# Two-token K/Q pieces, a mask added by TensorE and a new order, in sliding-window attention followed by a squared-ReLU MoE layer

## The chip, the cores and the metric

The kernel runs on one core of one Trainium2 chip. A core has TensorE (PE in the profile; PEld is its loading of weights), VectorE (DVE), ScalarE (ACT), GpSimd (POOL) and SyncE (SP). They run side by side and wait for each other by semaphores. Loads and stores go through 16 DMA engines, which all queues share. POOL, SP and ACT issue them; only those that POOL issues convert float32 to bfloat16 on the way here. The metric is the device time of one execution in microseconds (us), the median over runs.

## The reference

```python
def _attn_ref(q, k, v):                     # 8 batches, 8 heads, 576 tokens, 64 per head
    scores = scale * np.matmul(q, k.transpose(0, 1, 3, 2))          # scale = 1/8
    mask = np.abs(pos[:, None] - pos[None, :]) <= window            # window = 32
    scores = np.where(mask, scores, -1000000000.0)
    ...
    attn = attn / (np.sum(attn, axis=-1, keepdims=True) + 1e-09)    # softmax
    return np.matmul(attn, v)

def _moe_ref(x, w_in, w_out):               # x: 4608 x 512, w_in: 512 x 2048
    r = np.maximum(x @ w_in, 0.0)
    return (r * r) @ w_out
```

Attention gives 4608 tokens (8 batches of 576) with 512 features each, heads side by side, and these go through the two products. Inputs and output are float32.

## The kernel before

**Steps and tiles.** A batch is cut into nine steps of 64 queries, 72 steps in all. A step sees 128 keys, from 32 before its queries to 32 behind them. Its scores for all eight heads fill one PSUM bank, 128 keys by 512 (line 552; two banks, `sc`, taken in turn). ACT takes the exponential (line 562), DVE multiplies by a mask of 0 and 1 (line 569), PE multiplies with V (AV, line 585) where a column of ones beside V gives the sum, DVE divides (lines 597 and 599), and the result `xr` is turned into `xt`: by PE and ACT in the first 26 steps (lines 619 and 624), by a DMA afterwards (line 610).

Eight steps make a tile of 512 tokens, nine tiles in all. In a tile the first product, mm1 (line 629), makes the hidden layer in 16 units. A unit fills one of two PSUM banks, `ht`, in turn, so that a unit waits until ACT has taken the unit before the last from its bank; ACT applies the ReLU and DVE or ACT squares (lines 648 and 655), giving `gt`. From tile 2 on a unit is 128 features by 512 tokens, 8 matmuls of 64 rows. In tile 0 it is 256 features by 256 tokens, 16 matmuls, in the order of the list `UNITS`, whose entries are (first token, tokens, first block of 128 features); in tile 1 it is the same size, first half first. The second product, mm2 (line 662), goes through 128 tokens in four units of 8 matmuls, one for each fourth of the hidden layer (`seg`), into one of two banks, `outp`. Four loads bring w_in and four bring w_out, 512 hidden features each: blocks 0 to 3 of a unit's third entry need w_in chunk 0, and so on.

**How Q, K and V get in.** For batches 2 to 7, K and Q are loaded by heads (line 434), turned in blocks by DVE (line 492) and spread by SP's DMAs (line 506). Batches 0 and 1 take a faster way in `PIECES` of 128 tokens and a last one of 64: `fine_load` (line 388) puts one token of all heads on a partition, so that a run is 64 numbers; `fine_turn` turns it by PE with an identity (line 405), and ACT or DVE copy it from PSUM: K once (line 416), Q twice, each with half of the rows zeroed (lines 423 and 424). The first piece of batch 0 comes in float32 by SP's and ACT's queues into a part of `gt` not used yet, the others by POOL. V comes in four pieces of 128 tokens, shifted by 32, and two edges (lines 443 and 451); DVE makes a second copy for the even steps (line 463).

**What sets the order.** `Prog` records every operation with what it reads and writes, a key (its due time, in steps) and an estimated duration. Then `schedule` plays the program through and lets each engine, when it is free, take the ready operation with the smallest key. The order found is emitted as each engine's program; on the chip it is fixed, and an engine waits where an operation isn't ready. The keys come from the tables at the head: `LEAD`, `LB`, `TB`, `GB`, `QB`, `WB`, `VB` for the batches, `KM`, `TM`, `MD` for mm1 and mm2. `FIRST` lists the first 40 loads (K, Q, V, V edges, w_in as `a`, w_out as `b`) in the order in which POOL issues them, ahead of all others. `AHEAD` limits how many of POOL's loads may be under way: an issue waits for an earlier load where more than that many nanoseconds of transfer, by the plan's estimate, lie ahead. In time without other work PE multiplies a tile of zeros, `zz`, into an unused bank, to keep its clock up.

Of the kernel before, what the change touches and what calls it, by code (L numbers as in the profile page):

```python
# [5 lines left out]
ALU = mybir.AluOpType  # L6
ACTF = mybir.ActivationFunctionType
BF16 = mybir.dt.bfloat16
# [12 lines left out]
LEAD = 13  # L21
# [16 lines left out]
NG, GK = 72, -5.5  # L38
WIDE = (0,)
W1F = ()  # L40
QENG = 'AAAADDDDDA'
# [9 lines left out]
FIRST = (  # L51
# [6 lines left out]
)  # L58
WCH = ((0, 512), (512, 512), (1024, 512), (1536, 512))
PIECES = ((0, 128), (128, 128), (256, 128), (384, 128), (512, 64))  # L60
# [225 lines left out]
class Gen:  # L286
# [5 lines left out]
    def alloc(self):  # L292
# [14 lines left out]
        self.FR = {t: [sb(f"{t}fr{i}", [128, 5, H_, D_], BF16) for i in range(2)] for t in "qk"}  # L307
# [15 lines left out]
        self.FF = {t: wide[:, x:x + 1024].rearrange("p (x h d) -> p x h d", x=2, h=H_) for t, x in (("k", 2048), ("q", 3072))}  # L323
# [44 lines left out]

    def setup_rest(self, i, key):

        self.ms("DVE", [("vx0", i)], self.VX[i][64:96, 0, :, 0:64], 0.0, key, 280)
        self.ms("DVE", [("vx0", i)], self.VX[i][64:128, 0, :, 64:VS], 1.0, key, 80)
        self.ms("DVE", [("vx4", i)], self.VX[i][32:64, 4, :, 0:64], 0.0, key, 280)
        self.ms("DVE", [("vx4", i)], self.VX[i][0:64, 4, :, 64:VS], 1.0, key, 80)
# [5 lines left out]

    def fine_load(self, b, t, x, key):
        t0, n = PIECES[x]
        s = (self.q if t == "q" else self.k)[b][:, t0:t0 + n, :].rearrange("h p d -> p h d")
        d = self.FR[t][b][0:n, x, :, :]
        on = "POOL"
        if b == 0 and x in WIDE:
            d, on = self.FF[t][:, x, :, :], "ACT" if t == "q" else "SP"
        self.p.rec(on, lambda e: e.dma_start(d, s), writes=[("fraw", b, t, x)], dma=(f"f{b}{t}{x}", 0), key=key,  # L388
                   dur=(900 if n == 128 else 700) if on == "POOL" else 450, move=(n // 2, 14 if on == "POOL" else 16))

    def fine_turn(self, b, t, x, key):

        t0, n = PIECES[x]
        tag, ps = ("sc", t == "q"), self.SC[t == "q"]
        if b == 0 and x < 4:
            tag, ps = (("ht", x % 2), self.HT[x % 2][:]) if t == "q" else (("outp", 0), self.OUTP[0][:])
        wide = b == 0 and x in WIDE
        raw, ident, turned = (self.FF[t], self.IF, False) if wide else (self.FR[t][b], self.ID, n == 128)
# [10 lines left out]
        self.p.rec("PE", f, reads=[("fraw", b, t, x), "idf" if wide else "id"] + [("frz", b, t)] * (n < 128), writes=[tag], key=key,  # L409
                   dur=(232 if n == 128 else 120) * (4 if wide else 1),  # L410
                   mode="col")
        src = ps[:, 0:4 * n].rearrange("p (j c) -> p j c", j=4)
        if t == "k":
            dst = self.KT[b][:, :, 32 + t0:32 + t0 + n]
# [3 lines left out]
                       dur=(430 if n == 128 else 430) if on == "DVE" else (600 if n == 128 else 390))  # L418
            return
        for hm in range(2):  # L420
            dst, on = self.QZ[b][:, :, hm, t0:t0 + n], "DVE" if QENG[5 * b + x] == "D" else "ACT"
# [4 lines left out]
                       dur=(690 if n == 128 else 480) if on == "ACT" else (480 if n == 128 else 430))  # L426
# [29 lines left out]
    def copy_v(self, b, key, s0, s1):  # L456
# [4 lines left out]
        for r in (0, 64):  # L461
            dst, src = self.VX[i][r:r + 64, s0 + r // 64:s1 + r // 64, :, :], self.VD[i][r:r + 64, s0:s1, :, :]
# [33 lines left out]
    def spread(self, b, t, dh, key):  # L496
        st, i = self.ST[t], b % 2
        rd = [("st", t, dh, m0) for m0 in (0, 3, 5, 7)]
        old = [(t + "f", b - 2, x, hm) for x in range(5) for hm in range(2)] if b < 4 else []
# [10 lines left out]
    def qk_tags(self, b, c):  # L510
# [3 lines left out]
        if b < 2:  # L514
            for x in range((64 * c) // 128, min(575, 64 * c + 95) // 128 + 1):
                rd += [("kf", b, x, 0)]
# [299 lines left out]
```

## Time and profile before

| | us |
|---|---|
| median of three runs | 313.03 |
| the three runs | 310.76, 313.03, 314.44 |
| profiled execution | 312.9 |
| its span, first to last instruction | 311.1 |
| PE busy | 298.4 |
| DVE busy | 191.1 |
| ACT busy | 188.0 |
| POOL busy | 88.3 |

The granted TensorE clock was 1.000 over the span. The profile shows one execution. In its rows, "L67 PE MATMUL ht<-xt,w" is line 67 of the kernel, run on PE, that writes `ht` and reads `xt` and the weights; x and a number is how many there were. A row of a stretch of time gives the engine's busy time in it and the number of its instructions. In the page's second part a digit is a busy share in tenths for a fortieth of the span. Matmuls overlap, so that a busy PE isn't one at its peak.

### The profile page before, as it was taken

Reading aid. Unit: us, or ns where it says so; the run is one execution under the profiler, and the core shown is the slowest. Engines: PE = TensorE matmul, PEld = TensorE weight load, DVE = VectorE, ACT = ScalarE, POOL = GpSimd, SP = SyncE. Lnnn points to the kernel's source line nnn. Section 1 sums busy time; section 2 is a strip of 40 time slices with the busy share of each in tenths; the row PEclk is TensorE's granted clock in tenths of the full one; section 3 lists DMA queues with packets and bytes.
Section 4 is the critical chain, followed back from the end, with each engine's and each line's share of the span. In section 5 each row is a group of like instructions: output and inputs, shape, how many; then the busy total and the mean of one; then the engine's idle time right before and its main releaser. Section 6 shows DMA issues by size and latency. Waiting matters only on the chain.

```text
span 311.1 us, 9658 instructions
## 1 busy us (share of the span) xinstructions
PE 298.4 (96%) x4087; PEld 210.3 (68%) x4087; DVE 191.1 (61%) x485; ACT 188.0 (60%) x349; POOL 88.3 (28%) x127
## 2 busy tenths in 40 slices
PE   7799978999999999999999999999999999999996
PEld 3467967878867577677767776666666666565555
DVE  7865766877788788887858763869555440232000
ACT  3575776756746793588357868867786543253211
POOL 8837656973543242431141031000000000000000
PEclk9999999999999999999999999999999999999999
DMA  9999999999999979997799395434331110100112
GB/s 133 138 186 165 146 196 186 181 236 216 229 126 219 141 90 164 232 170 94 137 181 206 70 105 73 69 86 93 96 70 53 34 54 36 67 36 34 70 75 95
DMA packets 99226, 38.77 MB, mean 125 GB/s; under 512 B 71920, under 2 KB 94192, under 8 KB 99184
## 3 DMA queue, kind: packets, MB, share of 16 engines
q0 software_dynamic: 71584, 18.10, 63.1%
q1 hardware_dynamic: 21520, 10.63, 15.5%
q10 hardware_dynamic: 6080, 9.44, 9.9%
q8 instruction: 32, 0.52, 0.7%
q14 instruction: 10, 0.08, 0.1%
HBM read 36.70 MB, written 9.44 MB: 148 GB/s over the span
## 4 chain that ended last, share of the span: by engine, by line
PE 83%; DMA 9%; POOL 3%; issue 2%; ACT 1%; DVE 1%; SPq 0%; POOLq 0%; ACTq 0%
PE ht L67 38%; PE outp L67 37%; PE sc L552 4%; DMA xt<-xr 3%; PE ta L585 2%; DMA kfr<-in_k_dram 2%; DMA qz<-qst 2%; DMA qfr<-in_q_dram 2%; POOL vd L443 1%; POOL qfr L388 1%; POOL kfr L388 1%; ACT rt L648 1%; PE sc L405 1%; PE ta L619 1%; SPq L506 0%
## 5 line engine op out<-in xcount | busy, mean ns | idle before, releaser
L67 PE MATMUL ht<-xt,w 128*64 128x512 bf16 (+1 forms) x1408 | 140.5, 342 | 1.8 <-DMA xt<-xr 0.7
L67 PE MATMUL outp<-w,gt 128*64 128x512 bf16 (+1 forms) x1184 | 139.1, 373 | 0.0
L648 ACT ACTIVATE rt<-ht 128x512 bf16<-128x512 f32 x144 | 85.1, 596 | 56.7 <-PE ht L67 50.4
L67 PEld LDWEIGHTS ht<-xt,w 128*64 128x64 bf16 x1408 | 93.9, 137 | 31.5 <-issue 2.0
L67 PEld LDWEIGHTS outp<-w,gt 128*64 128x64 bf16 x1184 | 71.4, 110 | 38.2
L655 DVE TENSOR_TENSOR gt<-rt 128x512 bf16<-128x512 bf16 x94 | 38.9, 424 | 47.3 <-ACT rt L648 29.1
L562 ACT ACTIVATE e<-sc 128x512 bf16<-128x512 f32 x72 | 41.7, 598 | 8.6 <-PE sc L552 7.0
L676 ACT ACTIVATE oe<-outp 128x512 f32<-128x512 f32 x35 | 20.8, 595 | 37.7 <-PE outp L67 37.7
L443 POOL DMA_DIRECT2D vd<-in_v_dram x32 | 28.5, 893 | 45.7 <-PE ta L585 34.6
L492 DVE STREAM_TRANSPOSE qst<-qraw 128x256 bf16<-128x256 bf16 (+1 forms) x48 | 35.8, 830 | 1.7 <-DMA qz<-qst 1.7
L492 DVE STREAM_TRANSPOSE kst<-kraw 128x256 bf16<-128x256 bf16 (+1 forms) x48 | 35.9, 830 | 0.6 <-DMA kt<-kst 0.6
L597 DVE RECIPROCAL rs<-ta 128x4 f32<-128x4 f32 x72 | 13.0, 180 | 33.2 <-PE ta L585 32.7
L655 ACT ACTIVATE gt<-rt 128x512 bf16<-128x512 bf16 x50 | 31.6, 631 | 0.9
L569 DVE TENSOR_TENSOR pt<-e,mask 128x512 bf16<-128x512 bf16 x72 | 29.2, 410 | 4.4 <-ACT e L562 3.8
L599 DVE TENSOR_TENSOR xr<-ta,rs 128x256 bf16<-128x256 f32 x72 | 30.4, 422 | 0.9
L552 PE MATMUL sc<-qz,kt 128*64 128x128 bf16 x576 | 26.5, 219 | 2.6 <-issue 1.1
L552 PEld LDWEIGHTS sc<-qz,kt 128*64 128x64 bf16 x576 | 22.1, 110 | 8.1 <-issue 2.3
L434 POOL DMA_DIRECT2D qraw<-in_q_dram x24 | 15.2, 635 | 12.1 <-DVE qst L492 4.8
L451 POOL DMA_DIRECT2D vx<-in_v_dram x16 | 9.4, 590 | 27.1 <-PE ta L585 14.7
L434 POOL DMA_DIRECT2D kraw<-in_k_dram x24 | 14.5, 607 | 7.2 <-DVE kst L492 4.2
L463 DVE COPY vx<-vd 64x528 bf16<-64x528 bf16 (+1 forms) x28 | 14.7, 525 | 1.7 <-DMA vd<-in_v_dram 1.1
L585 PEld LDWEIGHTS ta<-vx,pt 128*64 128x64 bf16 x320 | 11.7, 111 | 5.2 <-issue 1.0
(53 smaller groups left out, 133.9 us busy)
## 6 DMA issues: line engine op xcount, KB each, us to landing
out_dram<-oe ACTq DMA_DIRECT2D x35, 256.0 KB, 3.1
vd<-in_v_dram POOLq DMA_DIRECT2D x32, 128.0 KB, 5.3
kraw<-in_k_dram POOLq DMA_DIRECT2D x24, 144.0 KB, 5.1
qraw<-in_q_dram POOLq DMA_DIRECT2D x24, 144.0 KB, 5.1
kt<-kst SPq DMA_DIRECT2D x48, 72.0 KB, 4.4
qz<-qst SPq DMA_DIRECT2D x48, 72.0 KB, 3.8
w<-in_moe_w_in_dram POOLq DMA_DIRECT2D x4, 512.0 KB, 8.4
w<-in_moe_w_out_dram POOLq DMA_DIRECT2D x4, 512.0 KB, 7.7
```

The lines of the kernel that those rows point to most:

```text
L67: mm = e.matmul(out[r:r + 64], w[:, r:r + 64], x, start=start, stop=stop)
L434: self.p.rec("POOL", lambda e, g=g, s=s: e.dma_start(raw[32 * g:32 * g + 32], s), writes=[("raw", t, b % 2, g)], dma=(f"{t}{b % 2}", b), k ...
L443: self.p.rec("POOL", lambda e, s=s: e.dma_start(self.VD[i][:, s, :, 0:64], v[b, :, 32 + 128 * s:160 + 128 * s, :].rearrange("h p d -> p h ...
L492: self.p.rec("DVE", lambda e: e.transpose(dst, src), reads=[("raw", t, i, g) for g in range(4)], writes=[("st", t, dh, m0)], key=key, dur= ...
L552: mm = e.matmul(sc[64 * u:64 * u + 64, 128 * j:128 * j + 128], self.KT[i][:, j, at:at + 64], self.QZ[i][:, j, :, 64 * c:64 * c + 64], star ...
L562: self.p.rec("ACT", lambda e: e.activation(ex, sc, ACTF.Exp, scale=0.125), reads=tags, writes=[("e", n % 4)], key=key, dur=600)
L569: self.p.rec("DVE", lambda e: e.tensor_tensor(pt, ee, mb, ALU.mult), reads=[("e", n % 4), ("mask", mi)], writes=[("pt", n % 4)], key=key, ...
L585: mm = e.matmul(self.PAIR[1][64 * u:64 * u + 64, 1, VE * j:VE * j + VE], pt[:, p0 + 64 * u * w:p0 + 64 * u * w + 64], vt[:, h, 0:VE], star ...
L599: self.p.rec("DVE", lambda e: e.tensor_tensor(bass.AP(xr, o, [[512, 128], [64, 4], [1, 64]]), bass.AP(self.PAIR[1], 512, [[1024, 128], [VE ...
L648: relu = self.p.rec("ACT", lambda e: e.activation(rt[:], ht[:], ACTF.Relu), reads=[("ht", k % 2)], writes=[("rt", k % 4)], key=key, dur=600)
L655: op = self.p.rec(on, lambda e: e.tensor_tensor(dst, rr, rr, ALU.mult) if on == "DVE" else e.activation(dst, rr, ACTF.Square), reads=[("rt ...
L676: self.p.rec("ACT", lambda e: e.activation(oe[:], op[:], ACTF.Copy), reads=[("outp", x % 2)], writes=[("oe", x % 3)], old=[("mtmp", 0), (" ...
```

## The change

K and Q of batches 0 and 1 come in three pieces of 128, 256 and 192 tokens. In the second and third a partition takes two tokens that follow each other, so a run is 128 numbers; PE turns the even and the odd tokens apart, and the copies from PSUM put them back in order. In the first nine steps (`NM`) PE writes a mask into the score bank first, 0 where a key is seen and −8e9 elsewhere (it is made from the masks by DVE and lies in `gt` until tile 1 needs the place), and adds the scores to it, so that the exponential gives the masked value at once and DVE's product is left out. The units of tile 1 have 512 tokens. The ones beside V are written once for all of `vx`, and the copies of V leave them alone. `FIRST`, `UNITS` and the tables of keys are new throughout.

```diff
-LEAD = 13
+LEAD = 2
...
-AHEAD = 5000
-LB = (-12.25, 1.5, 5.25, 2.5, 2.25, 10.75, 9.75, 11.25)
-TB = (22.5, -12.5, -8.5, -2.0, 13.0, 21.5)
-GB = (107.0, 61.0, 77.0, 134.0, 59.0, 9.0)
-TST, SK = 0.05, -10.5
-QB = (53.0, 15.0, -22.0, -4.0, 78.0, 126.0)
-WB = (-54.0, 16.0, 7.0, 75.0, 52.0, 128.0)
-VB = (43.5, -4.5, 36.5, -7.5, -19.0, 29.0)
-SQ = (12, 112, 2)
+AHEAD = 6000
+LB = (-8.5, -3.0, 3.25, 12.0, 1.75, 0.5, 7.0, 15.5)
+TB = (6.0, -7.5, -17.5, -25.0, 8.5, 67.5)
+GB = (223.0, 29.0, 45.0, 118.0, 26.0, 23.0)
+TST, SK = 0.15, -30.5
+QB = (24.0, -19.0, -63.0, 51.0, 51.0, 103.0)
+WB = (-31.0, 160.0, 81.0, 15.0, -4.0, 187.0)
+VB = (52.0, 3.0, 8.5, -58.5, 8.5, 24.5)
+SQ = (8, 112, 2)
...
+T1N = 512
+NM, MK = 9, 21.5
...
-FK, FQ = 41.75, 29.75
-VK0, VK1 = 5.75, 18.25
-KM, MD, TM = -34.5, 22.875, 4.0
+FK, FQ = 40.5, 15.0
+VK0, VK1 = -16.25, 1.0
+KM, MD, TM = -76.0, 21.625, 5.0
 UNITS = (
-    (256, 256, 4), (0, 256, 4), (256, 256, 0), (0, 256, 10), (256, 256, 8), (0, 256, 6), (256, 256, 2),
-    (0, 256, 0), (0, 256, 8), (256, 256, 6), (256, 256, 14), (0, 256, 2), (0, 256, 12), (256, 256, 12),
-    (256, 256, 10), (0, 256, 14),
+    (256, 256, 2), (0, 256, 4), (256, 256, 14), (256, 256, 4), (0, 256, 2), (0, 256, 0), (0, 256, 10),
+    (256, 256, 0), (0, 256, 6), (0, 256, 12), (256, 256, 10), (256, 256, 8), (0, 256, 8), (256, 256, 12),
+    (0, 256, 14), (256, 256, 6),
 )
 FIRST = (
-    ("q", 0, 1), ("v", 0, 1), ("q", 0, 3), ("v", 0, 2), ("v", 0, 3), ("k", 0, 1), ("e", 0, False),
-    ("v", 0, 0), ("q", 0, 4), ("k", 0, 2), ("q", 0, 2), ("q", 0, 0), ("k", 0, 3), ("q", 1, 1), ("a", 0, 1),
-    ("a", 0, 2), ("k", 0, 4), ("a", 0, 0), ("q", 1, 0), ("a", 0, 3), ("k", 1, 0), ("k", 1, 2), ("e", 0, True),
-    ("e", 1, False), ("v", 1, 1), ("v", 1, 0), ("k", 1, 4), ("k", 1, 1), ("b", 0, 1), ("q", 1, 2),
-    ("e", 1, True), ("v", 1, 2), ("k", 1, 3), ("b", 0, 0), ("b", 0, 2), ("q", 1, 3), ("k", 0, 0), ("b", 0, 3),
-    ("q", 1, 4), ("v", 1, 3),
+    ("e", 0, True), ("k", 1, 0), ("q", 0, 1), ("v", 0, 0), ("k", 0, 1), ("e", 0, False),
+    ("v", 0, 1), ("q", 0, 2), ("q", 1, 0), ("v", 0, 2), ("k", 0, 2), ("a", 0, 0), ("k", 0, 0),
+    ("v", 0, 3), ("a", 0, 1), ("e", 1, False), ("q", 1, 1), ("k", 1, 1), ("v", 1, 0),
+    ("a", 0, 3), ("b", 0, 0), ("v", 1, 2), ("q", 0, 0), ("b", 0, 3), ("a", 0, 2), ("q", 1, 2), ("v", 1, 1),
+    ("v", 1, 3), ("e", 1, True), ("k", 1, 2), ("b", 0, 1), ("b", 0, 2),
 )
...
-PIECES = ((0, 128), (128, 128), (256, 128), (384, 128), (512, 64))
+PIECES = (((0, 128, 1), (128, 256, 2), (384, 192, 2)), ((0, 128, 1), (128, 256, 2), (384, 192, 2)))
...
+    def setup_negs(self, key):
+        for i, (t, o) in enumerate(self.NEG):
+            dst = bass.AP(t, o, [[8192, 128], [1, 64]])
+            self.p.rec("DVE", lambda e, i=i, d=dst: e.tensor_scalar(d, self.MASK[i][:], -1.0, 8.0e9, ALU.add, ALU.mult),
+                       reads=[("mask", i)], writes=[("neg", i)], key=key, dur=90)
...
     def fine_load(self, b, t, x, key):
-        t0, n = PIECES[x]
-        s = (self.q if t == "q" else self.k)[b][:, t0:t0 + n, :].rearrange("h p d -> p h d")
+        t0, n, r = PIECES[b][x]
+        s = (self.q if t == "q" else self.k)[b][:, t0:t0 + n, :].rearrange("h (p r) d -> p h (r d)", r=r)
...
     def fine_turn(self, b, t, x, key):
...
         def f(e):
-            for j in range(4):
-                for u in range(2):
-                    h = 4 * (j // 2) + j % 2 + 2 * u
-                    mm = e.matmul(ps[64 * u:64 * u + 64, n * j:n * j + n], raw[:, x, h, :], ident[:, 0:n],
-                                  start=True, stop=True, is_transpose=turned)
+            for c in range(r):
+                for j in range(4):
+                    for u in range(2):
+                        h = 4 * (j // 2) + j % 2 + 2 * u
+                        o = m * (r * j + c)
+                        mm = e.matmul(ps[64 * u:64 * u + 64, o:o + m], raw[:, h, 64 * c:64 * c + 64], ident[:, 0:m],
+                                      start=True, stop=True, is_transpose=turned)
             return mm
...
-        src = ps[:, 0:4 * n].rearrange("p (j c) -> p j c", j=4)
+        src = ps[:, 0:4 * m * r].rearrange("p (j c i) -> p j i c", j=4, c=r)[:, :, 0:n // r, :]
...
     def copy_v(self, b, key, s0, s1):
...
-            dst, src = self.VX[i][r:r + 64, s0 + r // 64:s1 + r // 64, :, :], self.VD[i][r:r + 64, s0:s1, :, :]
+            dst, src = self.VX[i][r:r + 64, s0 + r // 64:s1 + r // 64, :, 0:64], self.VD[i][r:r + 64, s0:s1, :, 0:64]
...
     def scores(self, n):
...
+            if n < NM:
+                t, o = self.NEG[mi]
+                neg = bass.AP(t, o, [[8192, 128], [0, 8], [1, 64]])
+                self.p.rec("PE", lambda e: matmul(e, "col", sc.rearrange("p (h q) -> p h q", h=8), self.ID, neg, True, False),
+                           reads=["id", ("neg", mi)], writes=tags, key=key - MK, dur=240, move=2, mode="col")
...
-                                      self.QZ[i][:, j, :, 64 * c:64 * c + 64], start=True, stop=True)
+                                      self.QZ[i][:, j, :, 64 * c:64 * c + 64], start=n >= NM, stop=n >= NM or j == 3)
...
+        if n < NM:
+            pt = self.PT[n % 4][:]
+            self.p.rec("ACT", lambda e: e.activation(pt, sc, ACTF.Exp, scale=0.125),
+                       reads=tags, writes=[("pt", n % 4)], key=key, dur=600)
+            return
...
             key = 8 * T + d / 2 + TM - 8
-            if T == 1:
+            if T == 1 and T1N == 256:
                 self.mm1(T, 256 * (d // 8), 256, 2 * (d % 8), key)
```

More of the change, by code (lines that the diff above doesn't have):

```diff
@@ L386, in fine_load @@
-        if b == 0 and x in WIDE:
-            d, on = self.FF[t][:, x, :, :], "ACT" if t == "q" else "SP"
+        t0, n, r = PIECES[b][x]
+        s = (self.q if t == "q" else self.k)[b][:, t0:t0 + n, :].rearrange("h (p r) d -> p h (r d)", r=r)
+        d, on = self.piece(b, t, x)[0:n // r], "POOL"
+        if b == 0 and x in WIDE and r == 1:
+            d, on = self.FF[t], "ACT" if t == "q" else "SP"
         self.p.rec(on, lambda e: e.dma_start(d, s), writes=[("fraw", b, t, x)], dma=(f"f{b}{t}{x}", 0), key=key,
-                   dur=(900 if n == 128 else 700) if on == "POOL" else 450, move=(n // 2, 14 if on == "POOL" else 16))
+                   dur=(900 if n // r > 64 else 700) if on == "POOL" else 450,
+                   move=(n // r // 2, (14 if r == 1 else 22) + 2 * (on != "POOL")))
@@ L399, in fine_turn @@
+        turned = not wide and n != 64
+        m = n if n == 64 else 128
+        raw, ident = (self.FF[t], self.IF) if wide else (self.piece(b, t, x), self.ID)
         ps = ps.bitcast(BF16) if turned else ps
         def f(e):
-            for j in range(4):
-                for u in range(2):
-                    h = 4 * (j // 2) + j % 2 + 2 * u
-                    mm = e.matmul(ps[64 * u:64 * u + 64, n * j:n * j + n], raw[:, x, h, :], ident[:, 0:n],
-                                  start=True, stop=True, is_transpose=turned)
@@ L413, in fine_turn @@
+            return mm
+        self.p.rec("PE", f, reads=[("fraw", b, t, x), "idf" if wide else "id"] + [("frz", b, t)] * (n // r < 128), writes=[tag],
+                   key=key, dur=(232 * r if n > 64 else 120) * (4 if wide else 1), move=8 * r, mode="col")
+        src = ps[:, 0:4 * m * r].rearrange("p (j c i) -> p j i c", j=4, c=r)[:, :, 0:n // r, :]
         if t == "k":
-            dst = self.KT[b][:, :, 32 + t0:32 + t0 + n]
+            dst = self.KT[b][:, :, 32 + t0:32 + t0 + n].rearrange("p j (i c) -> p j i c", c=r)
@@ L498, in spread @@
         rd = [("st", t, dh, m0) for m0 in (0, 3, 5, 7)]
-        old = [(t + "f", b - 2, x, hm) for x in range(5) for hm in range(2)] if b < 4 else []
+        old = [(t + "f", b - 2, x, hm) for x in range(3) for hm in range(2)] if b < 4 else []
         for s in range(2):
@@ L656, in mm1 @@
                    reads=[("rt", k % 4)], writes=[("gt", T % 2, d0 + d, u) for d in range(nd) for u in us], key=key,
[L657 removed]
+                   old=["wf"] + [("fraw", 0, t, x) for t in "kq" for x in WIDE] + [("neg", i) for i in range(4)] if T == 1 else [],
                    dur=430 if on == "DVE" else 600)
@@ L757, in build @@
                     self.copy_v(1, n - LEAD - VK1, c, c + 1)
-                if b < 2 and (c % 2 or not c):
-                    x = (c + 1) // 2
-                    if x < 5:
+                for x, (t0, _, _) in enumerate(PIECES[b] if b < 2 else ()):
+                    if c == max(0, t0 // 64 - 1):
                         self.fine_turn(b, "k", x, n - LEAD - FK)
```

56 lines of the change are left out of this document (28 added, 28 removed).

## The prediction

> **What bounds the kernel now.** I read the page first, then the windows of the large matmuls, then the DMA and POOL rows of the start, then the waits and the chain. The page:
>
> ```profile
> PE 298.4 (96%) x4087; PEld 210.3 (68%) x4087; DVE 191.1 (61%) x485; ACT 188.0 (60%) x349; POOL 88.3 (28%) x127
> PE   7799978999999999999999999999999999999996
> DMA  9999999999999979997799395434331110100112
> ```
>
> PE is busy for 96% of 311.1 us, but not with products at first. Below, one row a stretch (length, PE busy, count in brackets, granted clock, DMA): the idle matmuls on the zero tile in the first row, and behind the dots all matmuls that touch the weights (both MoE products).
>
> ```profile
> 0.00:23.00 23.00, 10.92 (x55) 1.00 1.64 152
> ...
> 0.00:23.00 23.00, 1.18 (x18) 1.00 1.64 152
> 23.00:31.00 8.00, 4.84 (x80) 1.00 1.67 167
> 31.00:39.00 8.00, 6.93 (x118) 1.00 1.65 145
> 60.00:100.00 40.00, 37.86 (x420) 1.00 1.45 204
> 150.00:200.00 50.00, 46.50 (x397) 1.00 0.92 122
> ```
>
> Two stages. From 60 us on PE is the bound at a granted clock of 1.00. In the first 50 us it is fed by one stream of loads, and 18 products' matmuls fit into the first 23 us. The stream runs back to back: POOL issues (start, length), with the time from issue to landing of single ones beneath, in the order qfr, first w, second w, last vd.
>
> ```profile
> 1.35 1.02 POOL L388 DMA_DIRECT2D qfr<-in_q_dram  x1 [0.29 <-issue]
> 12.52 0.76 POOL L478 DMA_DIRECT2D w<-in_moe_w_in_dram  x1
> 13.73 0.74 POOL L478 DMA_DIRECT2D w<-in_moe_w_in_dram  x1 [0.45 <-DMA kfr<-in_k_dram]
> 45.42 0.89 POOL L443 DMA_DIRECT2D vd<-in_v_dram  x1
> ...
> qfr<-in_q_dram POOLq DMA_DIRECT2D x1, 128.0 KB, 5.1
> w<-in_moe_w_in_dram POOLq DMA_DIRECT2D x1, 512.0 KB, 7.7
> w<-in_moe_w_in_dram POOLq DMA_DIRECT2D x1, 512.0 KB, 9.0
> vd<-in_v_dram POOLq DMA_DIRECT2D x1, 128.0 KB, 6.5
> ```
>
> The first load lands at 1.35 + 5.1 = 6.45 us, the last of the list FIRST at 45.42 + 6.5 = 51.9: a stream of 45.5 us. A w_in chunk takes (13.73 + 9.0) − (12.52 + 7.7) = 2.5 us. The next two rows are the DMA packets of 6.5 to 13 us (nearly all one-token pieces, 128 bytes written to a packet) and of 46 to 60 us (mostly raw K/Q loads of four tokens, 512 bytes).
>
> ```profile
> DMA packets 7448, 0.94 MB, mean 144 GB/s; under 512 B 7448, under 2 KB 7448, under 8 KB 7448
> DMA packets 6036, 2.58 MB, mean 184 GB/s; under 512 B 2426, under 2 KB 5916, under 8 KB 6034
> ```
>
> A piece of 128 tokens is 1024 packets, so 7448 in 6.5 us are 0.89 us a piece. Price the old stream behind its first load: 21 such pieces (8 V, 13 K/Q) 18.7, four half pieces 1.8, four V edges of a quarter piece 0.9, eight weight chunks of equal size 20.0: 41.4 us. The measured 45.5 are 1.10 times that; I scale with it.
>
> **The change, part by part.** *Two-token pieces.* K and Q of batches 0 and 1 go from 18 POOL issues (this row and its like for Q) to 10.
>
> ```profile
> L388 POOL DMA_DIRECT2D kfr<-in_k_dram x9 | 7.9, 876 | 5.4 <-DMA qfr<-in_q_dram 2.8 <-DMA kfr<-in_k_dram 2.5
> ```
>
> That frees 8 × 0.88 us of POOL, which bounds nothing: ahead of these issues alone it sat 5.4 us, waiting for earlier loads to land (the limit on loads ahead). Full POOL time before 12.5 us hides behind loads that land every 0.9 us anyway. The two float pieces stay alone on SP's and ACT's queues.
>
> The gain is in the stream. All but the first 128 tokens of four tensors, 4 × 448 tokens × 1 KB = 1.83 MB, now move in 256-byte writes, which no row shows. Upper bound: as now, 0.89 us for 131 KB or 6.8 us/MB (0.131 MB), no gain. Lower bound: the weights' 2.5 us for 0.52 MB, 4.8 us/MB, a gain of 1.83 × 2.0 = 3.7. Between them lies the four-token row, 5.4 us/MB. If the time per byte is a constant plus a part that falls with the run (6.8 at 128 bytes, 5.4 at 512), it is 5.9 at 256: a gain of 1.83 × 0.9 = 1.7 us. I take 1.7, as the four-token row is the nearest; 256 tokens then cost 1.54 us and 192 cost 1.16. The Trainium skill ("DMA: Bandwidth & Descriptors", Specifications) puts the smallest transfer for full line rate at 512 bytes, which two-token reads just reach; by it the lower bound would hold. No row here shows a two-token load, so I keep that as a rival.
>
> *New order of loads.* With these prices times 1.10 from 6.45 us, the new FIRST lands (us): second K piece of batch 0 at 11.1, third at 16.9, w_in chunk 0 at 19.6, last V of batch 0 at 20.6, w_in 1 at 23.4, second K piece of batch 1 at 27.0, w_in 3 at 30.8, w_out 0 at 33.5, w_out 3 at 37.2, w_in 2 at 40.0, V piece 1 of batch 1 at 42.2, third K piece at 44.8, w_out 1 at 47.5, w_out 2 at 50.3. The end of the list moves from 51.9 to 50.3.
>
> What PE can do with it goes by these rows: the distance from start to start prices a step's score (0.22), turn of x (0.11) and AV (0.13), 0.46 us a step, an mm2 unit of 8 matmuls (0.86) and two mm1 units of 16 (1.75).
>
> ```profile
> 56.23 0.41 PE L552 MATMUL sc<-qz,kt 128*64 128x128 bf16 x8
> 56.45 0.30 PE L619 MATMUL ta<-ident,xr 128*64 128x128 bf16 x4
> 56.56 0.32 PE L585 MATMUL ta<-vd,pt 128*64 128x65 bf16 x8
> 56.69 1.05 PE L67 MATMUL outp<-w,gt 128*64 128x512 bf16 x8
> 57.55 1.94 PE L67 MATMUL ht<-xt,w 128*64 128x256 bf16 x32
> 59.30 1.05 PE L67 MATMUL outp<-w,gt 128*64 128x512 bf16 x8
> ```
>
> The units of tile 0 keep their order on each of the two ht banks. In the new UNITS only one unit of the first half tile stands ahead of units of the second half, so products begin when steps 4 to 7 are through, about 23 us (their last V lands at 20.6, then a copy, AV, turn). From 23 to 31 five units with chunks 0 and 1 can go; with chunk 3 three more, and with w_out 0 two mm2 units: 3 × 0.87 + 2 × 0.86 = 4.3 us of work for the 9 us from 31 to 40. Every other unit is chunk 2's or queued behind one of chunk 2. From 40 to 50.3 the other eight units (7.0), two turns of K and Q (0.9) and the seven steps held up by V piece 1 (3.2) fill PE. So by 50 us 18 units and 17 steps stand. What the old kernel had by then, all lines of PE from 0 to 50 us:
>
> ```profile
> L67 PE MATMUL ht<-xt,w 128*64 128x256 bf16 x264 | 16.8, 275 | 0.6 <-DMA w<-in_moe_w_in_dram 0.3 <-ACT rt L648 0.2
> L552 PE MATMUL sc<-qz,kt 128*64 128x128 bf16 x120 | 6.1, 221 | 1.9 <-issue 1.1 <-DVE kt L416 0.7
> L67 PE MATMUL outp<-w,gt 128*64 128x512 bf16 x24 | 3.1, 379 | 0.0
> ```
>
> That is 264 / 16 = 16.5 mm1 units, 24 / 8 = 3 mm2 units, 120 / 8 = 15 steps' scores, of which I count 14 done to the end: 1.5 units more than the new one (1.3 us) and three steps less (1.4 us). I take the two as even: the start as such brings nothing.
>
> *What follows the start.* All loads of later batches queue behind FIRST and come 1.6 us earlier. PE's waits from 50 to 300 us, and two pieces of the chain of waits:
>
> ```profile
> PE ht L67 <- DMA xt<-xr: 0.7, 1, 0.7
> PE sc L552 <- DMA qz<-qst: 0.7, 1, 0.7
> PE ta L585 <- issue: 0.7, 1, 0.7
> ...
> 100.99 6.16 DMA qz<-qst
> 154.02 3.85 DMA xt<-xr
> ```
>
> The two DMA waits, 1.4 us, are supply that came late by less than 1.6 us; I let them go. The bounds are 0 and, with the wait called issue, 2.1 us; the other way, new keys can bring as many new waits. What is late next is PE itself.
>
> *Mask by TensorE.* Nine steps lose a DVE product of 0.41 us and gain two matmuls of 512 columns.
>
> ```profile
> L569 DVE TENSOR_TENSOR pt<-e,mask 128x512 bf16<-128x512 bf16 x72 | 29.2, 410 | 4.4 <-ACT e L562 3.8
> L416 DVE COPY kt<-outp x3: 395/412/423, 12.1 to 17.2; 128x512 bf16<-128x512 bf16 x3
> L416 DVE CAST kt<-outp x1: 693/693/693, 9.4 to 9.4; 128x512 bf16<-128x512 f32 x1
> ```
>
> Eight matmuls of that width take 0.86 in an mm2 unit, so the pair costs 0.22 and nine pairs 1.9 us of PE, all before 23 us, where PE ran 10.92 us of idle matmuls: nothing. Without that cover it would be 1.9. The matmul waits for its score bank, with PE's next steps behind it, but its key puts it well ahead of the scores. The 3.7 us taken off DVE shorten each step by a hop, and the steps wait for K, V and w_in anyway: nothing. Four small DVE operations make the masks, below 1 us ahead of the first score.
>
> *Evacuating two-token pieces.* The K copy of 256 tokens takes the two tokens of a pair from places 128 elements apart: 2 × 0.41 if it runs like the bf16 copy above, 2 × 0.69 if like the f32 one. That is 0.6 us on the second K piece (landed 11.1) whose steps are through long before chunk 1 at 23.4: nothing. The V copies without the ones columns, the single memset of ones and the moved Q copies lie on DVE and ACT in the same shadow.
>
> *Tile 1 in 512-token units.* 16 units at 0.87 become 16 at 0.86: −0.2. They wait for step 15, whose K lands at 44.8; that is where the eight late units lie. Without them it would cost up to the 3 us until step 15 is through.
>
> **Sum.** The profiled execution took 312.9 us (span 311.1, and 1.8 around it), beside a median of 313.03. 312.9 − 0 (start even) − 1.4 (two waits on supply) − 0.2 (tile 1) = **311.3 us**.
>
> **The rivals.** *Stream at the weights' rate.* The pieces gain 3.7 × 1.10 = 4.0 us in place of 1.7 × 1.10: what lies at the end of the stream comes up to 2.2 us sooner and the dry stretch shrinks with it: 311.3 − 2.2 = 309.1, and down to 306 if the new order also rids PE of the issue wait (0.7) and of the 2.5 us that then are left dry. For it speaks that DMA is full until 150 us; against, that the four-token row stays at 184 GB/s.
>
> *Nothing comes through.* The later waits come back at other places: about 313. For it: from 60 us PE is full, and of the waits only 1.4 us are supply.
>
> *Slower: the dry stretch isn't made up.* PE works in a fixed order. Tile 0 runs out of units at about 31 + 4.3 = 35.3 us; if w_in chunk 2 lands later than that (I have 40.0) and the steps of batch 1 don't follow at once behind its units, the 4.7 us that PE stands dry are paid whole, since tile 1 can no longer start with its first half: 312.9 + 4.7 = 317.6. For it: chunk 2 stands behind w_out 0 and 3, which nothing needs so early. Against: 10 us of work are there from 40 on.
>
> **Chances.** A measurement of this kernel can tell about 1% from no change, 309.9 to 316.2 us. Forecast 0.42 (own range 309 to 313.5: 0.14 of it faster, 0.28 the same); weights' rate 0.28, faster; nothing 0.09, the same; dry stretch 0.21, of which 0.20 slower and 0.01 the same. Faster 0.42, same 0.38, slower 0.20. The range goes from 306.0, the low end of the second case, to 317.6, the last one's price: about half of the last case and a little of the second lie outside, some 15 to 20 in 100.
>
> **What would show it.** Right: the last load of FIRST lands near 50.3, w_in chunk 2 near 40, no MoE matmuls for some 4 us before it, PE full from 40 on, and no wait for xt or qz over 0.5 us after. A two-token piece of 256 tokens at 1.3 us or less speaks for the second case; over 1.7 for no gain in the stream. Wrong: new PE waits of several us after 60 us, or products beginning well before 20 us.

## The result, and the profile after

| | before | after |
|---|---|---|
| median, the two measured side by side | 312.49 us (310.11 to 316.22) | 312.94 us (311.8 to 314.81) |
| span of the profiled execution | 311.1 us | 311.9 us |

The ratio of after to before is 1.0058, with a 95% interval of 1.0034 to 1.0082: about 1.8 us slower. The ratio is taken from fast executions alone; the kernel before's median also counts slower ones, so the two medians lie closer together than the ratio says. The prediction had it 1.6 us faster (311.3 beside 312.9). The time lies in its range and within the 1% that it called the same; the sign is the wrong one. Times below come from different chips, so versions are compared by their ratios to the kernel before measured beside them; 1% is 3.1 us.

The page of the changed kernel, busy times and two of the rows of 40 slices (7.8 us each):

```profile
PE 300.4 (96%) x3981; PEld 206.2 (66%) x3981; DVE 188.9 (61%) x468; ACT 189.5 (61%) x347; POOL 81.5 (26%) x119
...
PE   4989999999999999999989999999999999999996
...
PEclk9799999999999999999999999999999999999999
```

The first slice has fallen from 7 tenths to 4, and the granted clock, 9 everywhere before, shows a 7 in the second. PE's waits over the whole span (total, times, longest) say what stands in the first slice:

```profile
PE sc L68 <- DVE gt L374: 4.0, 2, 3.5
PE ht L68 <- issue: 1.7, 2, 1.1
...
PE ht L68 <- DMA xt<-xr: 0.5, 2, 0.3
```

The first row is new. L68 into `sc` from `gt` is the mask matmul, L374 is the DVE operation of `setup_negs` that makes the mask it reads. The timeline of PE (start, length, and in brackets the idle time before and what ended it):

```profile
7.90 0.41 PE L68 MATMUL sc<-gt,ident 128*64 128x512 bf16 x2 [3.54 <-DVE gt L374]
8.77 0.64 PE L68 MATMUL sc<-gt,ident 128*64 128x512 bf16 x2 [0.47 <-DVE gt L374]
9.20 2.96 PE L68 MATMUL outp<-zz 128*64 128x512 bf16 x14
12.00 1.04 PE L420 MATMUL outp<-identf,gt 128*64 128x128 f32 x16
...
15.44 0.41 PE L574 MATMUL sc<-qz,kt 128*64 128x128 bf16 x8
```

PE takes its matmuls in the order written. The mask matmuls of steps 0 and 1 stand ahead of the first turns of K and Q, so these turns, whose loads were issued at 0.74 us and on their way for 3.9 and 4.7, start at 12.00. In the kernel before the same work was done here:

```profile
6.77 1.04 PE L405 MATMUL outp<-identf,gt 128*64 128x128 f32 x16
...
10.21 0.41 PE L552 MATMUL sc<-qz,kt 128*64 128x128 bf16 x8
```

The first score comes 5.2 us later (15.44 beside 10.21). What PE waited for, on DVE of the changed kernel, first its timeline, then its groups of 0 to 12 us (busy time, mean ns, idle time before):

```profile
4.98 1.21 DVE L364 COPY mask<-mask 64x64 bf16<-64x64 bf16 x3
...
6.35 0.90 DVE L364 COPY mask<-mask 64x64 bf16<-64x64 bf16 x3
7.28 0.56 DVE L374 TENSOR_SCALAR gt<-mask 128x64 bf16<-128x64 bf16 x1
...
8.02 0.72 DVE L374 TENSOR_SCALAR gt<-mask 128x64 bf16<-128x64 bf16 x3
```

```profile
L364 DVE COPY mask<-mask 64x64 bf16<-64x64 bf16 x6 | 2.0, 337 | 0.2
...
L374 DVE TENSOR_SCALAR gt<-mask 128x64 bf16<-128x64 bf16 x4 | 1.3, 472 | 0.1
```

The program that writes the order reckons 90 ns for each of these operations; they take 337 and 472 on average. The first turn of K has a smaller key (0 − 2 − 40.5 = −42.5) than the first mask matmul (0 − 2 − 8.5 − 21.5 = −32), so the mask can only have gone first because the plan had the masks ready while K was still on its way.

The wait has a second price. PE from 9 to 12 us (length, PE busy, granted clock, DMA, GB/s):

```profile
9.00:12.00 3.00, 3.00 (x17) 0.53 2.11 163
```

After 3.54 us without work the granted clock is 0.53 for the next 3 us, and the 14 idle matmuls written behind the masks take 12.00 − 9.20 = 2.8 us, 0.2 each; in the kernel before, 12 of them took 1.46 us, 0.12 each. The Trainium skill ("TensorE: Matmul & The Clock Gate", Part 1: The HAM clock gate) says that an idle window of about 3.4 us brings the array down to half rate; this row agrees.

Products in the same stretches as in the prediction:

```profile
0.00:23.00 23.00, 0.00 (x0) 0.93 1.58 167
23.00:31.00 8.00, 1.07 (x16) 1.00 1.47 201
31.00:39.00 8.00, 5.90 (x96) 1.00 1.60 188
...
60.00:100.00 40.00, 38.06 (x334) 1.00 1.12 174
```

Before 31 us stand 16 product matmuls, where the kernel before had 98. The stream of loads, on the other hand, ended far sooner than predicted. POOL's issues and the times from issue to landing of the list's last load and of chunk 2 of w_in (the second row of its pair), then of two 256-token pieces:

```profile
36.94 0.55 POOL L499 DMA_DIRECT2D w<-in_moe_w_out_dram  x1 [1.21 <-DMA w<-in_moe_w_in_dram]
...
26.84 0.76 POOL L493 DMA_DIRECT2D w<-in_moe_w_in_dram  x1
...
17.04 0.89 POOL L398 DMA_DIRECT2D qfr<-in_q_dram  x1
17.91 0.93 POOL L398 DMA_DIRECT2D kfr<-in_k_dram  x1
```

```profile
w<-in_moe_w_out_dram POOLq DMA_DIRECT2D x1, 512.0 KB, 9.3
...
w<-in_moe_w_in_dram POOLq DMA_DIRECT2D x1, 512.0 KB, 9.8
...
qfr<-in_q_dram POOLq DMA_DIRECT2D x1, 256.0 KB, 6.4
kfr<-in_k_dram POOLq DMA_DIRECT2D x1, 256.0 KB, 7.1
```

The last load lands at 36.94 + 9.3 = 46.2 us (51.9 before, 50.3 predicted), chunk 2 of w_in at 36.6 (40.0 predicted), and a 256-token piece takes (17.91 + 7.1) − (17.04 + 6.4) = 1.57 us.

So the question was whether the wait for the masks costs all that the faster stream brings, and what the other parts are worth.

### The profile page after: what moved, and what is told of

Its sections match the earlier page's. It is cut to its first block, busy times and chain, and to the rows that moved or that the text cites. A ratio compares the mean times of both kernels' runs of the same rounds, so it can differ in the third digit from the quotient of the medians.

```text
span 311.9 us, 9389 instructions
## 1 busy us (share of the span) xinstructions
PE 300.4 (96%) x3981; PEld 206.2 (66%) x3981; DVE 188.9 (61%) x468; ACT 189.5 (61%) x347; POOL 81.5 (26%) x119
## 4 chain that ended last, share of the span: by engine, by line
PE 89%; DVE 5%; DMA 4%; issue 1%; ACT 0%; ACTq 0%
PE ht L68 40%; PE outp L68 38%; PE sc L574 5%; DMA xt<-xr 4%; PE ta L611 3%; PE ta L645 1%; PE sc L420 1%; DVE qz L439 1%; PE sc L68 1%; DVE mask L364 1%; DVE xr L625 0%; PE outp L420 0%; PE ht L420 0%; DVE gt L374 0%; DVE kt L430 0%
## 5 line engine op out<-in xcount | busy, mean ns | idle before, releaser
L68 PE MATMUL ht<-xt,w 128*64 128x512 bf16 (+1 forms) x1280 | 139.8, 359 | 2.2 <-issue 1.7
L68 PE MATMUL outp<-w,gt 128*64 128x512 bf16 (+1 forms) x1184 | 139.8, 373 | 0.0
L68 PEld LDWEIGHTS ht<-xt,w 128*64 128x64 bf16 x1280 | 90.4, 137 | 34.0 <-issue 3.1
L68 PEld LDWEIGHTS outp<-w,gt 128*64 128x64 bf16 x1184 | 69.0, 110 | 39.3
L589 ACT ACTIVATE e<-sc 128x512 bf16<-128x512 f32 x63 | 36.8, 598 | 8.5 <-PE sc L574 7.9
L458 POOL DMA_DIRECT2D vd<-in_v_dram x32 | 28.5, 895 | 46.2 <-PE ta L611 31.8
L507 DVE STREAM_TRANSPOSE kst<-kraw 128x256 bf16<-128x256 bf16 (+1 forms) x48 | 37.0, 823 | 1.0 <-DMA kt<-kst 1.0
L595 DVE TENSOR_TENSOR pt<-e,mask 128x512 bf16<-128x512 bf16 x63 | 25.8, 413 | 13.3 <-ACT e L589 13.0
L681 ACT ACTIVATE gt<-rt 128x512 bf16<-128x512 bf16 x52 | 32.9, 632 | 0.8
L574 PE MATMUL sc<-qz,kt 128*64 128x128 bf16 x576 | 27.3, 219 | 0.6 <-DVE kt L430 0.5
L478 DVE COPY vx<-vd 64x512 bf16<-64x512 bf16 (+1 forms) x28 | 13.6, 485 | 1.9 <-issue 1.0
L650 ACT ACTIVATE xt<-ta 128x256 bf16<-128x256 bf16 x26 | 10.0, 384 | 7.4 <-PE ta L645 7.2
```

What stands on the lines that cost most here:

```text
L68: mm = e.matmul(out[r:r + 64], w[:, r:r + 64], x, start=start, stop=stop)
L458: self.p.rec("POOL", lambda e, s=s: e.dma_start(self.VD[i][:, s, :, 0:64], v[b, :, 32 + 128 * s:160 + 128 * s, :].rearrange("h p d -> p h ...
L478: self.p.rec(on, lambda e, d=dst, c=src: e.tensor_copy(d, c) if on == "DVE" else e.activation(d, c, ACTF.Copy), reads=rd, writes=[("vxc", ...
L507: self.p.rec("DVE", lambda e: e.transpose(dst, src), reads=[("raw", t, i, g) for g in range(4)], writes=[("st", t, dh, m0)], key=key, dur= ...
L574: mm = e.matmul(sc[64 * u:64 * u + 64, 128 * j:128 * j + 128], self.KT[i][:, j, at:at + 64], self.QZ[i][:, j, :, 64 * c:64 * c + 64], star ...
L589: self.p.rec("ACT", lambda e: e.activation(ex, sc, ACTF.Exp, scale=0.125), reads=tags, writes=[("e", n % 4)], key=key, dur=600)
```

## The experiments

*Late masks.* The list of PE is made as in the changed kernel; then the mask matmuls of steps 0 and 1 are moved to just ahead of their scores, and the idle matmuls are filled in afterwards. The order on all other engines is the same.

```diff
         for m, x in self.late:
+            m.start = x.start - 0.001
...
-            self.p.rec("PE", f, reads=self.qk_tags(b, c) + tags * (n < NM), writes=tags, key=key, dur=230, mode="col")
+            self.p.late += [(self.p.ops[-1], self.p.rec("PE", f, ...))][:n < 2]
```

> The kernel after, with the mask matmuls of steps 0 and 1 moved on TensorE to just ahead of their scores; DVE, ACT, POOL and SP keep their order word for word. Theory A (TensorE stood still for masks that DVE made late, 3.5 and 0.5 us, then ran its planned idle matmuls late, so that the start is some 5 us behind): the first turn comes at about 6.5 us in place of 12.0, the first product at about 23 in place of 27.0, and the time falls by 2 to 4 us, to 309 to 311, a ratio to before of about 0.99. Rival B (the loads set the start, whatever TensorE does at 8 us): first product still at 26 to 27 us, time as after, 312.5 to 313.5. Rival C (the 1.9 us of added mask matmuls are what is paid): no change either.

Measured: 308.63 us (307.87 to 309.5), ratio 0.9924 (0.9895 to 0.9953). That is 1.0058 − 0.9924 = 1.3%, or 4.2 us, faster than the changed kernel, and it beats the kernel before too. PE's timeline and its longest wait:

```profile
5.26 1.09 PE L420 MATMUL outp<-identf,gt 128*64 128x128 f32 x16
...
9.35 0.38 PE L68 MATMUL sc<-gt,ident 128*64 128x512 bf16 x2
11.65 0.41 PE L574 MATMUL sc<-qz,kt 128*64 128x128 bf16 x8 [1.92 <-DVE kt L430]
```

The first turn starts at 5.26 in place of 12.00, the first score at 11.65 in place of 15.44, and the wait for the masks is gone. The place of the two matmuls, with the idle matmuls that are filled in around them, was worth 4.2 us.

*No idle matmuls behind the wait.* The changed kernel without the 14 idle matmuls that follow the masks; the masks stay where they are.

```diff
-            for k in range(int((gap - 60) // one)):
+            for k in range(int((gap - 60) // one) if at < 4000 or at > 9000 else 0):
```

> The kernel after without the 14 idle matmuls that stand between the early mask matmuls and the first turn; the wait for DVE's masks stays. Theory A: the first turn moves from 12.0 to about 9.3 us, half of what the stall costs, and the time falls by 1 to 2 us. Rival B: no change. If it falls as far as with the masks moved, the idle matmuls alone are the price and the wait none.

Measured: 310.48 us (309.78 to 311.6), ratio 0.9996 (0.9971 to 1.0022). That is 0.6% or 1.9 us off the changed kernel (0.8 to 3 by the two intervals); the other half of the 4.2 us is the wait itself. They weren't a pure loss:

```profile
9.21 1.92 PE L420 MATMUL outp<-identf,gt 128*64 128x128 f32 x16
10.91 1.92 PE L420 MATMUL ht<-identf,gt 128*64 128x128 f32 x16
...
14.51 0.39 PE L574 MATMUL sc<-qz,kt 128*64 128x128 bf16 x8
```

Without them the first turn starts 2.8 us sooner, but each turn takes 10.91 − 9.21 = 1.70 us from start to start where the kernel before took 0.87, so the score comes only 0.9 us sooner. In both versions the array runs slow after the wait: idle matmuls at 0.2 us each in the one, f32 turns at 1.70 us in the other.

*Mask on DVE, order made anew.*

```diff
-NM, MK = 9, 21.5
+NM, MK = 0, 21.5
```

> The kernel after with the mask multiplied by DVE in all 72 steps again (no mask matmuls, no mask tiles of -8e9); the plan is made anew, so that orders on all engines differ somewhat. Theory A: no stall at 4 to 9 us, first product at about 23 us, time 309 to 312, near that of the masks moved. Rival C: 1.9 us below after and the moved masks no better than after. Rival B: as after.

Measured: 311.75 us (310.58 to 312.37), ratio 1.0017 (0.9993 to 1.0041): 0.4% better than the changed kernel, 0.9% behind the late masks. The wait for the masks is gone here too, but the whole order is a different one, so this run alone can't say what the mask's place on DVE costs.

*Mask on DVE, order kept.* Nine multiplications on DVE are put in behind their exponentials, the mask matmuls are taken out, and everything else stays in the order of the late masks (DVE still makes TensorE's masks of −8e9, though nothing reads them here).

```diff
+            out.remove(m)
+            w.eng, w.fn, w.deps = "DVE", fn, {ex}
+            w.start, w.dur = ex.start + ex.dur + 1, 430
+            out.append(w)
```

> The version with the late masks, in which the mask of the first nine steps is multiplied in by DVE after the exponential, as before the change, with everything else in the same order (the mask matmuls are taken out of the list, nine multiplications of 0.43 us are put in behind their exponentials). If the mask matmuls are at nothing once they stand behind the turns, as the prediction put it, the time stays within 0.5 us of 308.6. If they pay for a shorter chain (each step without DVE's 0.43 us and its hand-over), it rises by 0.5 to 2 us. If they cost their own 1.9 us of PE, it falls by 0.5 to 1.9.

Measured: 309.66 us (309.11 to 310.9), ratio 0.9951 (0.9926 to 0.9975), 0.27% or 0.8 us above the late masks; the two intervals overlap, so the size isn't settled. Its PE shows two waits for DVE between 0 and 80 us that the late masks don't have there:

```profile
PE ta L665 <- DVE xr L645: 0.9, 1, 0.9
PE ta L629 <- DVE pt L605: 0.8, 1, 0.8
```

The first product starts at 24.7 us, where the late masks have 22.7. So once the mask matmuls stand behind the turns, their 1.9 us of PE cost no more than the shorter steps bring; the run doesn't price the two apart.

*No zeroing.* With the late masks, DVE's list still ends the wait ahead of the first score. This version drops the four fills of unused rows; the turns read 96 rows.

```diff
-        mm = e.matmul(..., raw[:, h, 64 * c:64 * c + 64], ident[:, 0:m], ...)
+        mm = e.matmul(..., raw[0:w, h, 64 * c:64 * c + 64], ident[0:w, 0:w], ...)
...
-                self.ms("DVE", [("frz", b, t)], self.piece(b, t, 2)[...], 0.0, K + 5, 300)
```

> The version with the late masks, without the four fills of the unused rows of the last two-token pieces on DVE (0.48 us each, 1.9 us in all ahead of the first K copy); their turns read 96 rows instead of 128. If DVE's own list of set-up work is what now ends the wait ahead of the first score (1.9 us in the version with the late masks), the first score stands 1.5 to 2 us earlier, near 10 us, the wait for DVE's K copy is below 0.5 us, and of that at most 1 us reaches the end: 307.6 to 308.6. If the first products wait for the weights and not for the steps, the time doesn't move, within 0.4 us.

Measured: 308.92 us (307.34 to 309.8), ratio 0.9915 (0.9887 to 0.9943): no difference. The first score comes 1.7 us sooner (9.93 in place of 11.65), and its waits, two of them before 80 us and the last one behind, say where that went:

```profile
9.93 0.39 PE L575 MATMUL sc<-qz,kt 128*64 128x128 bf16 x8
...
PE ht L68 <- DMA w<-in_moe_w_in_dram: 0.9, 1, 0.9
...
PE sc L575 <- DVE kt L431: 0.2, 1, 0.2
...
PE ta L612 <- DVE xr L626: 1.6, 1, 1.6
```

The wait for DVE's K copy falls from 2.2 us to 0.2. A wait of 0.9 for w_in, which the late masks didn't have, and one of 1.6 for a step's result after 80 us, where they have 0.2, stand in its place. By these rows of one execution, an earlier first score is worth something only while nothing else is late.

*One-token runs.* The late masks, with each two-token piece loaded by two issues of one-token runs; the order is kept.

```diff
+        for c in range(r):
+            self.p.rec(on, lambda e, c=c: e.dma_start(d[:, :, 64 * c:64 * c + 64], s[:, :, 64 * c:64 * c + 64]), ...)
```

> The version with the late masks (308.63 us), in which each two-token piece is loaded by two issues, each with runs of one token (128 bytes), as before the change; the plan's order is kept. If the longer runs themselves gain what the prediction priced for them, the last load of the first list lands about 1.7 us later than the 46.2 us of the changed kernel, near 48, POOL has 8 issues more at 0.7 us each, and the time rises by 0.5 to 1.7 us, to 309.1 to 310.3. If the earlier end of the stream came from something else, it lands within 0.5 us of 46.2 and the time stays within 0.5 us. If runs of one token move at the rate of the old kernel's whole stream, it lands 3.5 us or more later and the time is 311 or more.

Measured: 313.06 us (311.56 to 313.47), ratio 1.0055 (1.0031 to 1.0078), 1.3% or 4.1 us above the late masks. The issue and the latency of the last load of the list, in the late masks and here:

```profile
37.45 0.55 POOL L499 DMA_DIRECT2D w<-in_moe_w_out_dram  x1 [1.19 <-DMA w<-in_moe_w_in_dram]
...
w<-in_moe_w_out_dram POOLq DMA_DIRECT2D x1, 512.0 KB, 8.8
```

```profile
40.71 0.55 POOL L499 DMA_DIRECT2D w<-in_moe_w_out_dram  x1 [0.69 <-DMA w<-in_moe_w_in_dram]
...
w<-in_moe_w_out_dram POOLq DMA_DIRECT2D x1, 512.0 KB, 9.0
```

It lands at 49.7 in place of 46.2. With the same order of loads the long runs bring 3.5 us of the stream, and about as much of the time. (The version also has eight issues of POOL more; their share wasn't measured by itself.)

*One-token runs, order made anew* with the durations of these loads in the plan:

> As the version with one-token runs (313.06 us), but the plan is made anew with the durations of these loads. If the 4.4 us that it lost to the version with the late masks were the price of a stale order, it comes back to within 1.5 us of 308.6. If they are the price of the stream, it stays at 311.5 or more, with the last load of the first list at 49 us or later.

Measured: 315.08 us (314.55 to 316.38), ratio 1.0156 (1.0116 to 1.0196). The last load lands at about 52 us. So the loss doesn't come back with a new order; the new one is 1% worse still. It is one order among many, though, and doesn't rule out that another would do better.

*Tile 1 in halves,* in the changed kernel and with the late masks. The order is made anew from about 45 us on.

```diff
-T1N = 512
+T1N = 256
```

> The kernel after with tile 1 in units of 256 tokens again (the plan is made anew from some 45 us on). I priced this part at 0.2 us, by 16 units of 0.87 in place of 0.86: all theories expect the time of after within 0.5 us, 312.5 to 313.5. A change of over 1 us means that waiting for all eight steps of tile 1 counts.

> The version with the late masks, with tile 1 in 256-token units; the plan is made anew from there on, as in the earlier run with tile 1 in halves (317.43, +5.7 us over its list). If tile 1 in halves costs by itself, the same 4 to 6 us appear again: 312.5 to 314.5. If the loss of the earlier run was its plan's luck with its start, this one stands within 1.5 us of 308.6. The prediction's own term was 0.2 us.

Measured: 317.43 us (316.32 to 319.43), ratio 1.0229 (1.0182 to 1.0276), 1.7% above the changed kernel; and 312.19 us (311.31 to 315.76), ratio 1.0046 (1.0013 to 1.0078), 1.2% above the late masks. Both are far over the 0.2 us that the prediction gave this edit. PE's waits of 80 to 180 us in the second:

```profile
PE ht L68 <- issue: 2.1, 1, 2.1
PE ht L68 <- ACT xt L650: 0.7, 1, 0.7
PE ta L611 <- DVE xr L625: 0.7, 1, 0.7
PE ta L611 <- DVE pt L595: 0.6, 1, 0.6
```

That is 4.1 us of waits, where the late masks have 0.6 in this stretch. None is tile 1's own: both waits at `ht` stand ahead of units of 512 tokens, which tile 1 doesn't have here. Three of the four are operations standing too close behind a step of attention; for the longest the profile shows no cause. This raised the suspicion that the order, and not the part, was at fault, so three runs went from the kernel before.

*Tile 1 in 512-token units alone,* in the kernel before (its `if T == 1` never taken):

> The kernel before with tile 1 in 512-token units, everything else as it was (the plan is made anew from there on). By the prediction's term (16 units at 0.86 in place of 16 at 0.87) the time moves by 0.2 us; by the two runs with halves in the changed kernel, which lost 3.5 to 4.5 us in waits for attention steps at 80 to 180 us, it falls by up to 3.5, to 307.5. The kernel before lost only 1.4 us to such waits there, so a fall by more than 1.5 would have to come from elsewhere.

Measured: 314.44 us (313.54 to 316.38), ratio 1.0146 (1.0103 to 1.0189). Halves are worse in the new kernel, whole units are worse in the old one.

*Two-token pieces alone,* in the old order, with the old keys, masks on DVE and tile 1 in halves:

> The kernel before with one part of the change alone: two-token pieces of K and Q for batches 0 and 1, in the old order of loads (each long piece where the first of its halves stood), with the old keys and units, the masks on DVE and tile 1 in halves. If the longer runs gain what the version with one-token runs lost (its stream ended 3.5 us later), the last load of the first list lands near 48.4 in place of 51.9. If such a gain reaches the end by itself, the time is 307 to 309.5 beside the kernel before's 311. If the old order can't use it, because longer pieces bring the first steps' K and Q later and the first products wait for them, the time is 310.5 or more and the first products start no sooner than 20.9 us.

Measured: 316.69 us (314.1 to 319.39), ratio 1.0185 (1.0133 to 1.0238). The last load of the list landed at 49.0 us (51.9 before), and the time rose by 5.7 us. PE's waits from 80 us on:

```profile
PE ta L607 <- DVE pt L591: 3.1, 2, 2.2
PE sc L570 <- DMA qz<-qst: 1.4, 1, 1.4
PE ht L64 <- DMA xt<-xr: 1.4, 1, 1.4
PE ta L641 <- DVE xr L621: 1.3, 1, 1.3
```

These are 7.2 us of waits in the later steps. The numbers of the last case held (the first product starts at 22.2 us, 1.3 later than before), but its reason covers 1.3 us at most; the larger part was lost after 80 us.

*The order alone.* The kernel before, without any change to an operation; the planner is told 630 ns for an exponential in place of 600.

```diff
-                   reads=tags, writes=[("e", n % 4)], key=key, dur=600)
+                   reads=tags, writes=[("e", n % 4)], key=key, dur=630)
```

> The kernel before with not one operation changed; only the length that the planner assumes for an exponential is 630 ns in place of 600, so that the order of work is made anew. If the 3.5 to 6 us that the versions with one part exchanged lost (tile 1 in halves or whole, two-token pieces alone, one-token runs replanned) are the price of an order that the keys were not made for, this one loses too: 313 to 317, with new waits of PE for pt, xr or xt at 80 to 180 us. If those losses come from the exchanged parts, this one stays within 1 us of the kernel before.

Measured: 312.15 us (310.67 to 314.91), ratio 1.0049 (1.0011 to 1.0087). An order made anew costs 0.5% here with not one operation changed. That is a loss, as the first case had it, but under its 313 us, and without the new waits that it named: PE's waits after 80 us come to 1.6 us, those of the kernel before to 1.7. One such draw doesn't tell how much of the 1.0 to 1.9% of the others is the order and how much the part.

## Why the prediction was wrong

**The step that failed** is the one on the mask: "The matmul waits for its score bank, with PE's next steps behind it, but its key puts it well ahead of the scores", and, of DVE's operations, "below 1 us ahead of the first score". It asked who waits behind the matmul and looked only at the score bank. The other thing the matmul reads, the mask, was priced by its length and not by the time at which DVE has it done. Well ahead of the scores was also ahead of the turns. The kernel before's trace had the number that was needed: DVE's mask copies, from which the new masks are made, ran until 6.04 + 0.90 = 6.9 us there, while PE's turns began before 6.8. In the changed kernel the first mask was done at 7.28 + 0.56 = 7.8 us, and the turns could have begun at 5.3, as the late masks show.

```profile
4.47 1.41 DVE L362 COPY mask<-mask 64x64 bf16<-64x64 bf16 x3
...
6.04 0.90 DVE L362 COPY mask<-mask 64x64 bf16<-64x64 bf16 x3
```

Priced at nothing, the step cost 4.2 us, as the late masks show: more than the 1.6 us that the prediction expected from everything. 1.9 of it (0.8 to 3) went through the idle matmuls behind the wait at a granted clock of 0.53, which no step had. With the masks late the kernel is 0.76% or 2.4 us faster than the one before, the way that the prediction had it; that this lies near its 1.6 is in part luck, as its other terms were off too. The Trainium skill ("TensorE: Matmul & The Clock Gate", Part 2: What happens when you issue a matmul) says that matmuls stay in program order and only weight loads are pulled ahead; the turns that stood ready behind the masks agree.

**What bounds the kernel**: right. PE is full from 60 us on, and what the late masks save ahead of the first score (3.8 us) comes out at the end. The next 1.7 us, saved by leaving out the zeroing, did not.

**Two-token pieces**: the mechanism was right, the size too small. The gain of the stream is 3.5 us, not 1.7, over 1.83 MB, 1.9 us/MB where the lower bound had 2.0. The four-token row, chosen as the nearest, was the wrong guide; the rival at the weights' rate had the price. The 512 bytes of the Trainium skill for full line rate ("DMA: Bandwidth & Descriptors", Specifications) fit this gain, counted by the bytes read (two tokens are 512). A single piece read off two landings took 1.57 us, near the 1.54 that the prediction gave it: the test by a piece's duration that the prediction offered would have misled. Either a piece's landing doesn't tell what the whole stream gains, or one-token pieces cost more here than the 0.89 us of before; no run tells which. The factor of 1.10 on all loads did not come back: without it the predicted list comes to (50.3 − 6.45) / 1.10 = 39.9 us behind the first load, and it ended 46.2 − 6.2 = 40.0 us behind it (that load was issued at 1.34 and took 4.9 us). The match is luck in part: the version with one-token runs ended 49.7 − 6.5 = 43.2 us behind its first load, where these prices without a gain come to 39.9 + 1.7 = 41.6. So prices 4 to 5% too low and a gain 1.8 us too small cancelled.

**Start even, with a dry stretch**: wrong in both halves. Chunk 2 landed at 36.6, not 40.0, and from 31 to 39 us the products filled 5.90 us (7.51 with the late masks), not the 4.3 in 9 us. But PE came to it late: the first product stands at 27 us in place of 23. With the late masks it is at 22.7, so that forecast was good for a kernel without the wait. Neither of the signs of being wrong that the prediction named, long waits after 60 us and products well before 20, appeared.

**Later waits**: in part. The two DMA waits of 1.4 us fell to 0.5; but PE waits 1.1 us called issue after 50 us stand beside them.

**Evacuating two-token pieces**: hidden but for half a microsecond, and in the slower half of its bounds (0.82 to 1.38): DVE took 1.22 us for the 256-token K copy, and PE waited 0.5 us for it.

**Tile 1**: the 0.2 us could not be seen. No run changes tile 1 with the order held.

**The sum** as a method had a gap of its own. "New keys can bring as many new waits" stood in it as one clause. Of seven versions with an order made anew, one of them with no part changed, six lie 0.5 to 2.3% above the kernel before, and the mask on DVE lies level with it. What the order is worth by itself in the change isn't settled: with the order held, the masks' place cost 4.2 us and the long runs (with eight issues fewer) brought 4.1. If the two add up to nothing, most of the 1.8 us that the change lost, and the gain of the mask on TensorE if it has one, fall on the new order, the units and tile 1 together, and no run here divides them.

## What to carry to other kernels

When an operation is put ahead of others on an engine that works in order, ask of each of its inputs at what time it is ready, by the trace, and not only how long it takes to make. Small set-up operations planned at 90 ns and lasting 340 to 470 on average were enough here to hold the first matmuls for 3.5 us. And in a kernel whose order is written by a program, exchange parts with the order held, as done here for the masks and the loads: a part exchanged with a new order shows the order as much as the part.

## What was not expected of the hardware

After PE had stood for 3.54 us, the f32 turns took 1.70 us from start to start in place of 0.87, in a run where the granted clock of that stretch is recorded as full:

```profile
9.00:12.00 3.00, 3.00 (x30) 1.00 2.13 166
```

This is the version without the idle matmuls; with them the record shows 0.53. So in these two runs a matmul's own duration was the safer sign of a slow array than the clock's record. And tiny operations on DVE are not cheap by their size: the 64x64 mask copies took 174 to 628 ns, the longest being three and a half times the shortest for the same shape.
